# Local attention and a feed-forward block on one core: split values, means and maxima go through a buffer in HBM, and four more chunks use seven block products

## The chip, the cores and the metric

The kernel runs on one core of a Trainium2 chip. The metric is the device time of one execution in microseconds (us): the median of 3 runs is 672.36 us (671.85 to 673.94). Beside them stands one execution under the profiler. The five engines are called as in the profile: PE multiplies matrices (PEld is its weight load), DVE, ACT and POOL work on vectors, and SP issues the DMA transfers of this kernel, one after the other.

## The reference

The inputs are q, k, v with 4 batches, 8 heads, 768 positions and 64 columns a head, and two weights. Per head, each query attends to the keys closer than 16 positions and, without a mask, to one maximum of the keys and one mean of the values for every block of 32. The heads side by side are then the 512 columns of 3072 tokens of a feed-forward block.

```
k_sum = k.reshape(B, H, nb, 32, D).max(axis=3)
v_sum = v.reshape(B, H, nb, 32, D).mean(axis=3)
scores = concat([where(|i - j| < 16, scale*q@k.T, -1e9), scale*q@k_sum.T + log(32)])
a = softmax(scores)                      # over keys and block maxima together
x = a @ concat([v, v_sum])               # (B, H, S, D) -> (3072, 512)
h = x @ w_in                             # 512 -> 2048
out = (h * sigmoid(h)) @ w_out           # 2048 -> 512
```

## The kernel before

**Number format.** Chunk 0 of the tokens multiplies in float32. Everything later is scaled by a power of two and split into two float16 parts, high and low, and each product is three float16 matmuls (high by high, high by low, low by high). The scale comes from a maximum over all 128 partitions: `all_max`, a reduction on POOL over the partitions. It is used once for the weights (`w_scale`), once per batch for the values (`v_scale`) and once each for batches 1 to 3 for queries and keys (`job_scale`).

**Attention.** The 3072 tokens are 24 tiles `s` of 128 queries, 6 to a batch. A tile goes through `job_qk` (load and split q and k), `job_scores` (PE, line 605), `job_a` (softmax on DVE and ACT, then four DMA transposes, line 691, that turn the probabilities), `job_c` (PE, line 724, the product with the values) and `job_x` (split x). For `job_c` each half tile `z` of 64 queries needs one tile `vv` in SBUF with 96 rows of local values and 24 rows of block means, each row 512 columns high and 512 low in float16, 2 KB. In batches 1 to 3, which are 18 tiles, `job_vn` loads 256 rows of v, splits them on ACT or DVE (lines 545 to 547) into one of two slots `vn`, and `job_vs` then copies rows from the slots and from `vmp` (the means) to `vv` by eight DMAs from SBUF to SBUF, all issued at line 574: of 15, 81, 79 and 17 rows, and four of 24 rows. A slot can be written again when the copies that read it have landed.

**Feed-forward.** Twelve chunks of 256 tokens. A chunk takes the 2048 hidden columns in eight pairs of 128. In chunks 1 to 9 a pair (`job_f`) is 24 matmuls of 256 columns (line 838), a chain of ACT and DVE (lines 863 to 867) and 12 matmuls of 512 columns (line 851). In chunks 10 and 11 (`FAST = 10`) the second product of a pair (`job_fast`) is made of seven block products with 21 matmuls of 256 columns (line 968). For it, DVE or POOL form four sums of 128 columns (line 953), and two more splits follow (lines 949, 950, 955, 956).

**Order.** A planner (`Plan`) receives every operation with its engine, cost, buffers and priority, sweeps through them with modelled latencies and writes one fixed order per engine. Each engine works through its list in that order, so an instruction that waits holds back all that stand behind it on its engine. Attention for chunk `c + 2` is placed among the products of chunk `c`. The table `TUNE` shifts the priorities. Where the planner sees PE idle early or ahead of a first product it puts in matmuls on an identity (line 337).

Of the kernel before, what the change touches and what calls it, by code (L numbers as in the profile page):

```python
# [10 lines left out]
F32 = mybir.dt.float32  # L11
# [45 lines left out]
NSUP = 2  # L57
FAST = 10
EARLY = 40
ALLMAX = 1100  # L60
PACE = 4
# [6 lines left out]
class Plan:  # L68
# [58 lines left out]
    def sweep(self, prio, on, back):  # L127
# [18 lines left out]
        while ready:  # L146
# [13 lines left out]
            if e == "pe" and not back:  # L160
                early = early and cols < self.BUSY
# [12 lines left out]
            else:  # L174
                stop = t + cost * (1.0 if e in ("pe", "dma") else self.MARGIN)
# [58 lines left out]
def local_attn_ffn(ctx: ExitStack, tc: tile.TileContext, qkT, qP, qF, kF, v, vR, vP, w, out):  # L234
# [17 lines left out]
    const = ctx.enter_context(tc.tile_pool(name="const", bufs=1))  # L252
    psum = ctx.enter_context(tc.tile_pool(name="psum", bufs=1, space=bass.MemoryType.PSUM))

# [50 lines left out]
    v0_t = ring(2, [P, 2 * DM], F32, "v0")  # L305
    vn_t = [t.bitcast(F16).rearrange("p (a i c) -> p a i c", a=2, i=2) for t in v0_t]
    vmf_t = const.tile([P, 4, P], F16, name="vmf")
    nc.gpsimd.memset(vmf_t, 0.0)
# [28 lines left out]
    plan = Plan(tc, lambda: nc.tensor.matmul(out=bank[0][:, :2 * P], lhsT=unit[:, :P], rhs=unit, start=True, stop=True))  # L337
    count = {}

    def nxt(tag, n):  # L340
# [16 lines left out]
    def bk(k):  # L357
        return [("bank", k, half) for half in range(2)]
# [33 lines left out]
    def job_scale(b, prio):  # L392
# [8 lines left out]
        qs = qsc_t[b % 2]  # L401
        plan.op({"pool": ALLMAX}, lambda e: all_max(qc[:, 0:2], qm_t[:, 7:9]), r=["qm_q", "qm_k"], w=["qc"], prio=prio)
        steps = (
# [9 lines left out]
    def job_km(b, prio):  # L413
# [30 lines left out]
    def job_v(b, prio):  # L444
# [14 lines left out]
        plan.op({"dve": 180}, lambda e: nc.vector.scalar_tensor_tensor(out=lo, in0=vm_t, scalar=by, in1=hi, op0=ALU.mult, op1=ALU.subtract), r=need, w=["vmf"], prio=prio)  # L459
        plan.op({"dma": 1250}, lambda e: nc.sync.dma_start_transpose(out=vmp_t, in_=vmf_t.rearrange("p a b -> p (a b)")), r=["vmf"], w=["vmp"], prio=prio)  # L460

# [77 lines left out]
    def job_vn(b, n, prio):  # L539
# [6 lines left out]
                nc.vector.tensor_scalar(out=vn[:, :, 0], in0=flat, scalar1=vsc[:, 0:1], scalar2=None, op0=ALU.mult), r=key + [("vsc", b % 2)], w=vn_key(g % 2), prio=prio)  # L546
        plan.op({"dve": 1196}, lambda e: nc.vector.scalar_tensor_tensor(out=vn[:, :, 1], in0=flat, scalar=vsc[:, 0:1], in1=vn[:, :, 0], op0=ALU.mult, op1=ALU.subtract), r=key + [("vsc", b % 2)], w=vn_key(g % 2), prio=prio)

    def job_vs(s, prio):
        prio += nudge("vs", s)  # L550
        b, t = divmod(s, NTILE)
        if b == 0:
            return
        if t == 0:
            job_vn(b, 0, prio)
            job_vn(b, 1, prio)
        if t == 3:
            job_vn(b, 2, prio)
        vv = vv_t[s % 2]
        key = ("vv", s % 2)  # L560

        def rows(z, at, tile, first, n):
            if not 0 <= tile < NTILE:
                return vv[at:at + n, z].rearrange("p i c -> p (i c)").bitcast(F32), v[0, t if z == 0 else NTILE - 1, at:at + n, z, :]
            g = (b - 1) * (NTILE // 2) + tile // 2
            return vv[at:at + n, z], vn_t[g % 2][first:first + n, tile % 2]
# [9 lines left out]
        slots = {((b - 1) * (NTILE // 2) + x // 2) % 2 for x in (t - 1, t, t + 1) if 0 <= x < NTILE}  # L576
        plan.op({"dma": 2100}, load, r=["vmp", "first"] + [k for x in slots for k in vn_key(x)], w=[key], prio=prio)

# [44 lines left out]
    def job_a(m, prio):  # L623
# [55 lines left out]
        for j, n in enumerate(ns):  # L679
# [10 lines left out]
            plan.op({"dve": 510}, low, r=[sum_key(j, i) for i in range(2)] + [("e", n, i) for i in range(2)], w=pkeys, prio=prio)  # L690
            plan.op({"dma": 1250}, lambda e, tt=tt, pt=pt: nc.sync.dma_start_transpose(out=tt, in_=pt.rearrange("p a b -> p (a b)")), r=pkeys + ["third"], w=[ttk], prio=prio)

# [98 lines left out]
    def w_scale(prio):  # L791
        plan.op({"dve": 80}, lambda e: nc.vector.tensor_reduce(out=wx_t, in_=wm_t, axis=AX.X, op=ALU.max), r=[("wm", f, kind) for f in range(NFT) for kind in range(2)], w=["wx"], prio=prio)
        plan.op({"pool": ALLMAX}, lambda e: all_max(wc[:, 0:2], wx_t), r=["wx"], w=["wc"], prio=prio)
        steps = (
# [18 lines left out]
    def job_f(n, c, fs):  # L813
# [11 lines left out]

        def fill():
            nc.tensor.matmul(out=h[:, :CH], lhsT=unit[:, :P], rhs=unit, start=True, stop=True)

        def ffn1(at, f, cs):
# [25 lines left out]
        for at, f in enumerate(fs):  # L855
            need = [("wf", f, 0)] if c == 0 else [("wh", f, 0), ("wl", f, 0)]
            if n < HALVES:
                for half in range(2):
                    cs = slice(half * P, half * P + P)
                    plan.op({"pe": 900}, ffn1(at, f, cs), r=[("xh", z, half), ("xl", z, half)] + need, w=[("bank", k, half)], prio=i, cols=2048, fill=fill)  # L860
            else:
                plan.op({"pe": 1800 if c == 0 else 1312}, ffn1(at, f, slice(0, CH)), r=xs + need + turn, w=bk(k) if at == 0 else [("bank", k, 1)], prio=i + at, cols=4096 if c == 0 else 3072, fill=fill)
        plan.op({"act": 51 + 213 * m if c == 0 else 147 + 213 * m}, lambda e: nc.scalar.activation(out=t, in_=h, func=AF.Tanh, scale=0.5 if c == 0 else th[:, 0:1]), r=bk(k) + ([("th", b % 2)] if c else []) + free, w=tk, prio=post)  # L863
# [65 lines left out]
    def job_fast(n, c, fs):  # L929
# [6 lines left out]

        def fill():
            nc.tensor.matmul(out=h[:, :CH], lhsT=unit[:, :P], rhs=unit, start=True, stop=True)

        for at, y in enumerate(fs):  # L940
            plan.op({"pe": 1312}, ffn1_pairs(h, at, y, z), r=[(x, z, half) for x in ("xh", "xl") for half in range(2)] + [("wh", y, 0), ("wl", y, 0), ("turn", n - 3)], w=bk(k) if at == 0 else [("bank", k, 1)], prio=i + at, cols=3072, fill=fill)
        t = area(4 * j + 3, 0, F32)
# [70 lines left out]
    def job_tail(n, c, fs):  # L1013
# [8 lines left out]

        def fill():
            nc.tensor.matmul(out=h[:, :CH], lhsT=unit[:, :P], rhs=unit, start=True, stop=True)

        for at, f in enumerate(fs):
            plan.op({"pe": 1312}, ffn1_pairs(h, at, f, z), r=[(x, z, half) for x in ("xh", "xl") for half in range(2)] + [("wh", f, 0), ("wl", f, 0), ("turn", n - 3)], w=bk(k) if at == 0 else [("bank", k, 1)], prio=i + at, cols=3072, fill=fill)
        for at in range(2):
# [130 lines left out]

TUNE = dict(quad=308.75, vd=-86.5, ws=818.0, s0=-738.75, wp=1594.25, wm=33.0, km=-55.75, w_dma=-1.5, w_dec=878.75, a0=-71.0, a1=-119.25, d1=-66.5, span=51.75, post=1866.5, ffn2=5.0, jc0=92.5, jc1=-1748.25, jx0=2.25, jx1=143.0, vs=617.5, qk=305.75, k=-1369.75, v=-54.75, v0=83.75, out=-4.5, first=1452.5)  # L1160

# [60 lines left out]
```

## Time and profile before

| | before |
|---|---|
| median of 3 runs | 672.36 us |
| profiled execution, device time | 674.95 us |
| its span, first to last instruction | 673.2 us |
| PE busy | 598.7 us, 89% |
| DVE busy | 458.7 us, 68% |
| ACT busy | 342.6 us, 51% |
| POOL busy | 92.9 us, 14% |
| mean granted PE clock | 0.953 of full speed |

The span is what the rows below divide; the device time of the same execution is 1.75 us longer. A busy PE need not work at its peak, since the granted clock may be at its lower level. The three stages used later are the start with chunks 0 and 1 (0 to 126 us), chunks 2 to 9 with most of the attention (126 to 584 us), and chunks 10 and 11 (584 us to the end).

### The profile page before, as it was taken

To read this page: it belongs to the slowest core of one execution; us is meant where nothing else is said; L and a number is where in the kernel's file an instruction comes from. 1 tells how busy PE (TensorE), PEld (TensorE's weight loads), DVE (VectorE), ACT (ScalarE), POOL (GpSimd) and SP (SyncE) were. 2 spreads that over 40 slices of the span, in tenths; PEclk is the share of its full clock that TensorE was granted. 3 is DMA by queue.
4 is the path that set the end of the run, shared out by engine and by line. 5 is a ranking of instruction groups with operands and counts; after the bars stand their busy time and mean duration, and the time that the engine had idled before them with its cause. 6 is when DMAs were issued, how large, how long until landed. Compare 5 with 4: busy or idle time off the path is not lost.

```text
span 673.2 us, 15159 instructions
## 1 busy us (share of the span) xinstructions
PE 598.7 (89%) x5944; PEld 413.3 (61%) x5944; DVE 458.7 (68%) x1243; ACT 342.6 (51%) x837; POOL 92.9 (14%) x183
## 2 busy tenths in 40 slices
PE   8899999799749858996998876999996798999997
PEld 5667666466526525663665543666663566688886
DVE  6799897898074636982773643879857696255655
ACT  4899885565054541651554532545643554234342
POOL 4112002201000000000000000005222420031130
PEclk9999999799969969998999797999997899999999
DMA  8997612237544539636433536474473379000000
GB/s 342 417 418 284 201 56 87 77 101 92 117 129 124 118 123 140 157 81 83 127 98 101 144 72 97 109 183 44 141 78 103 46 88 80 1 32 1 33 1 31
DMA packets 64938, 80.07 MB, mean 119 GB/s; under 512 B 44068, under 2 KB 46052, under 8 KB 63076
## 3 DMA queue, kind: packets, MB, share of 16 engines
q1 hardware_dynamic: 64868, 79.12, 48.0%
q8 instruction: 46, 0.75, 0.5%
q14 instruction: 24, 0.20, 0.1%
HBM read 54.33 MB, written 6.29 MB: 90 GB/s over the span
## 4 chain that ended last, share of the span: by engine, by line
PE 46%; DMA 21%; DVE 15%; ACT 9%; SPq 4%; issue 4%; POOL 0%; DVEq 0%; ACTq 0%
PE bank L851 16%; PE bank L838 15%; DMA first<-v 9%; PE bank L926 6%; DMA raw<-in_qF_dram 6%; PE bank L968 5%; SPq L574 3%; DMA third<-first 2%; DVE wr L789 2%; ACT e L644 2%; DVE wr L773 2%; PE bank L724 1%; PE bank L605 1%; ACT wr L866 1%; DVE first L688 1%
## 5 line engine op out<-in xcount | busy, mean ns | idle before, releaser
L851 PE MATMUL bank<-wr 128*128 128x512 f16 x768 | 193.1, 400 | 52.6 <-ACT wr L866 45.2
L838 PE MATMUL bank<-x,wr 128*128 128x256 f16 x1728 | 205.2, 275 | 1.3 <-DVE work L864 1.3
L838 PEld LDWEIGHTS <-wr 128*128 128x128 f16 x1728 | 169.3, 99 | 38.8 <-issue 3.7
L851 PEld LDWEIGHTS <-wr 128*128 128x128 f16 x768 | 75.0, 101 | 140.3 <-ACT wr L866 47.2
L864 DVE SCALAR_TENSOR_TENSOR wr<-wr,bank 128x512 f32<-128x512 f32 x64 | 43.7, 683 | 67.0 <-ACT wr L863 66.7
L644 ACT ACTIVATE e<-e,mx 128x120 f32<-128x120 f32 x192 | 73.2, 384 | 17.4 <-DVE mx L641 17.3
L863 ACT ACTIVATE wr<-bank,th 128x512 f32<-128x512 f32 x64 | 43.5, 679 | 69.2 <-PE bank L838 69.2
L866 ACT ACTIVATE wr<-wr 128x512 f16<-128x512 f32 x64 | 40.1, 627 | 49.4 <-DVE wr L864 49.3
L867 DVE SCALAR_TENSOR_TENSOR wr<-wr 128x512 f16<-128x512 f32 x64 | 45.9, 717 | 16.1 <-ACT wr L866 15.7
L688 DVE SCALAR_TENSOR_TENSOR first<-e,sum,first 128x120 f16<-128x120 f32 x144 | 44.9, 363 | 4.3 <-POOL first L657 4.1
L657 POOL TENSOR_SCALAR first<-e,sum 128x120 f16<-128x120 f32 x33 | 14.9, 455 | 238.2 <-DVE sum L650 56.4
L926 PE MATMUL bank<-x,wr 128*128 128x256 f16 x384 | 45.8, 273 | 0.1
L641 DVE CUSTOM_DVE_ANT_0 e<-bank,masks,qsc 128x120 f32<-128x120 f32 x144 | 40.2, 338 | 4.5 <-PE bank L605 4.5
L926 PEld LDWEIGHTS <-wr 128*128 128x128 f16 x384 | 37.5, 98 | 5.5 <-issue 0.3
L968 PE MATMUL bank<-wr 128*128 128x256 f16 x315 | 37.7, 273 | 0.0
L644 ACT ACTIVATION_READ_ACCUMULATOR e<-e,mx 128x1 f32 x192 | 36.5, 190 | 0.0
L968 PEld LDWEIGHTS <-wr 128*128 128x128 f16 x315 | 30.7, 98 | 3.6
L848 PE MATMUL bank<-wr,work 128*128 128x512 f32 x64 | 29.2, 594 | 1.6 <-DVE work L864 1.6
L835 PE MATMUL bank<-x,wr 128*128 128x256 f32 (+1 forms) x144 | 29.8, 359 | 0.4 <-issue 0.4
L953 POOL TENSOR_TENSOR wr<-wr 128x128 f32<-128x128 f32 x33 | 18.8, 573 | 76.0 <-DVE wr L953 71.0
L250 POOL TENSOR_TENSOR wr<-wr 128x256 f32<-128x256 f32 x32 | 25.8, 823 | 20.4 <-DVE wr L911 11.6
L851 PE MATMUL bank<-wr,work 128*128 128x512 f16 x96 | 24.2, 395 | 4.7 <-ACT work L866 2.7
(153 smaller groups left out, 760.8 us busy)
## 6 DMA issues: line engine op xcount, KB each, us to landing
wr<-in_w_dram SPq DMA_DIRECT2D x14, 1024.0 KB
raw<-in_qkT_dram SPq DMA_DIRECT2D x18, 576.0 KB
out_dram<-raw SPq DMA_DIRECT2D x23, 256.0 KB
raw<-in_kF_dram SPq DMA_DIRECT2D x12, 384.0 KB
raw<-in_qF_dram SPq DMA_DIRECT2D x9, 512.0 KB
raw<-in_vR_dram SPq DMA_DIRECT2D x12, 384.0 KB
raw<-in_vP_dram SPq DMA_DIRECT2D x9, 512.0 KB
first<-v SPq DMA_DIRECT2D x18, 162.0 KB
```

The lines of the kernel that those rows point to most:

```text
L641: plan.op({"dve": 262 if b else 206}, lambda e, i=i, j=j, et=et, mx=mx: nc.vector.tensor_tensor_reduce(out=et[:, i, :], in0=sc[j][:, i, :N ...
L644: plan.op({"act": 385}, lambda e, i=i, j=j, et=et, mx=mx: nc.scalar.activation(out=et[:, i, :], in_=et[:, i, :], func=AF.Exp, scale=-1.0, ...
L688: nc.vector.scalar_tensor_tensor(out=pt[:, i, P:P + NKEY], in0=et[:, i, :], scalar=su4[:, 2 * j + i:2 * j + i + 1], in1=pt[:, i, :NKEY], o ...
L835: nc.tensor.matmul(out=o, lhsT=wi[:, ct * P:(ct + 1) * P], rhs=x0[:, ct, cs], start=(ct == 0), stop=(ct == NCT - 1))
L838: nc.tensor.matmul(out=o, lhsT=wip[:, part, ct * P:(ct + 1) * P], rhs=x[:, ct, :], start=(ct == 0 and q == 0), stop=(ct == NCT - 1 and q = ...
L851: nc.tensor.matmul(out=bank[ob[u]][:, cs], lhsT=g[:, rows], rhs=wop[:, part, cs], start=(begins and q == 0), stop=(stops and q == 2))
L863: plan.op({"act": 51 + 213 * m if c == 0 else 147 + 213 * m}, lambda e: nc.scalar.activation(out=t, in_=h, func=AF.Tanh, scale=0.5 if c == ...
L864: plan.op({"dve": 70 + 267 * m}, lambda e: nc.vector.scalar_tensor_tensor(out=t, in0=t, scalar=1.0, in1=h, op0=ALU.add, op1=ALU.mult), r=b ...
L866: plan.op({"act": 98 + 213 * m}, lambda e: nc.scalar.activation(out=gh, in_=t, func=AF.Copy, scale=SHRINK), r=tk + free, w=ghk, prio=post)
L867: plan.op({"dve": 76 + 267 * m}, lambda e: nc.vector.scalar_tensor_tensor(out=gl, in0=t, scalar=SHRINK, in1=gh, op0=ALU.mult, op1=ALU.subt ...
L926: nc.tensor.matmul(out=h[:, at * CH:at * CH + CH], lhsT=wip[:, p, ct * P:(ct + 1) * P], rhs=x[:, ct, :], start=(ct == 0 and q == 0), stop= ...
L968: nc.tensor.matmul(out=acc_of(c, m)[0], lhsT=x[:, left[m]], rhs=right[m](p), start=(opens and q == 0 and m in (1, 4, 2, 7)), stop=(closes ...
```

## The change

- **Values.** After the split, `job_vn` stores 256 rows from its slot to `vd` in HBM (line 564). `job_vs` then reads the local rows of each half tile from there with one DMA of up to 96 rows (line 592), so two per tile in place of four. The means are stored once per batch to `md` in HBM by `keep` (two DMAs, line 474) and read into each of the two `vv` buffers once per batch (line 581).
- **Maxima.** `all_max` no longer runs on POOL. It stores the 128 partitions' values to `sd` in HBM (line 430), reads them back into every partition (line 431) and reduces on DVE (line 432). This is done eight times.
- **Chunks.** `FAST = 6`: chunks 6 to 9 also take their second product by seven block products.
- **Order.** Some costs given to the planner change, its rule for early identity matmuls changes, and `TUNE` has other numbers, so the order of all engines is another one.

```
-FAST = 10
+FAST = 6
...
-    def all_max(out, in_):
-        nc.gpsimd.partition_all_reduce(out, in_, P, bass_isa.ReduceOp.max)
...
+    def all_max(out, in_, r, w, prio):
+        i, n = nxt("sd", 2 * B), in_.shape[1]
+        flat, row = sd_t[i].rearrange("p n -> (p n)")[:n * P], vms_t[:, :n * P]
+        plan.op({"dma": 600}, lambda e: nc.sync.dma_start(out=flat.rearrange("(p n) -> p n", n=n), in_=in_), r=r, w=[("sd", i)], prio=prio)
+        plan.op({"dma": 450}, lambda e: nc.sync.dma_start(out=row, in_=flat.unsqueeze(0).to_broadcast([P, n * P])), r=[("sd", i)], w=[("vms", 0)], prio=prio)
+        plan.op({"dve": 65 + 133 * n}, lambda e: nc.vector.tensor_reduce(out=out, in_=row.rearrange("q (p n) -> q n p", n=n), axis=AX.X, op=ALU.max), r=[("vms", 0)], w=w, prio=prio, port=())
...
+        def keep(e):
+            for i in range(2):
+                nc.sync.dma_start(out=md_t[b - 1][:, i], in_=vmp_t[i * BLK:i * BLK + NB].rearrange("p a b -> p (a b)"))
...
+        plan.op({"dma": 1300}, lambda e: nc.sync.dma_start(out=vd_t[b - 1][n * 2 * P:(n + 1) * 2 * P].rearrange("(a p) i c -> p a i c", a=2), in_=vn), r=vn_key(g % 2), w=[("vd", b, n)], prio=prio)
...
-        part = P - HALF + HALO
-        moves = [rows(0, NB, t - 1, P - HALO, HALO), rows(0, NB + HALO, t, 0, part + 2), rows(1, 0, t, HALF - HALO, part), rows(1, part, t + 1, 0, HALO + 2)]
-        moves += [(vv[rowsm[z], z, i], vmp_t[i * BLK:i * BLK + NB].rearrange("p a b -> p (a b)")) for z in range(2) for i in range(2)]
...
-            for o, i in moves:
-                nc.sync.dma_start(out=o, in_=i)
...
-        plan.op({"dma": 2100}, load, r=["vmp", "first"] + [k for x in slots for k in vn_key(x)], w=[key], prio=prio)
...
+            a = t * P + z * HALF - HALO
+            lo, hi = max(a, 0), min(a + NKEY - NB, S)
+            spans.append((local[z].start + lo - a, lo, hi))
...
+            for z, (at, lo, hi) in enumerate(spans):
+                nc.sync.dma_start(out=vv[at:at + hi - lo, z], in_=vd_t[b - 1][lo:hi])
...
+        plan.op({"dma": 1050}, load, r=[("vd", b, n) for n in units] + ["first"], w=[key], prio=prio)
```

On SP, this is what one tile's copies look like before, about a third of the way through (`v_125` and `v_126` are the two slots, `first` holds `vv`, and the last number of rows times 1024 columns is the size):

```order
L691 DMA_TRANSPOSE third<-first 128x4x128 x4
L574 DMA first<-v_126 15x1024
L574 DMA first<-v_126 81x1024
L574 DMA first<-v_126 79x1024
L574 DMA first<-v_125 17x1024
L574 DMA first<-vmp 24x512 x4
L377 DMA raw_117<-in_kF_dram 128x768
L397 DMA raw_116<-in_qF_dram 128x1024
```

And here is SP after, at the end of the first of the three batches, where the maxima for the next batch pass through HBM (`sd`) and the last tile of the batch reads its rows from `vd`:

```order
L430 DMA sd_139<-qm 128x2
L431 DMA vms<-sd_139 128x256
L592 DMA first<-vd_129 96x1024
L592 DMA first<-vd_129 79x1024
L459 DMA raw_120<-in_vR_dram 128x768
L709 DMA_TRANSPOSE third<-first 128x4x128
L459 DMA raw_120<-in_vR_dram 128x768
L709 DMA_TRANSPOSE third<-first 128x4x128 x3
```

Eight issues for a tile have become two. Over the program SP issues 30 loads of 96 rows, 3 of 81 and 3 of 79; one of 79 is the last tile of each batch, whose halo ends at the last position.

The other place is DVE at the scale of the weights. Before, `wc` comes straight behind `wx`, from POOL:

```order
L864 SCALAR_TENSOR_TENSOR work<-work,bank_170 128x512
L792 TENSOR_REDUCE wx<-wm 128x2
L795 TENSOR_SCALAR wc<-wc 128x2
L796 TENSOR_SCALAR wc<-wc 128x2
L797 TENSOR_SCALAR ws<-wc 128x2
L798 RECIPROCAL ws<-ws 128x2
```

After, five instructions of other work stand between `wx` and the reduction that reads the values back:

```order
L810 TENSOR_REDUCE wx<-wm 128x2
L381 TENSOR_REDUCE km_151<-raw_119 128x24
L760 SCALAR_TENSOR_TENSOR x_182<-bank_192,vsc_157,x_182 128x4x128
L381 TENSOR_REDUCE km_151<-raw_120 128x24
L879 SCALAR_TENSOR_TENSOR work<-work,bank_185 128x512
L381 TENSOR_REDUCE km_151<-raw_119 128x24
L432 TENSOR_REDUCE wc<-vms 128x2
L813 TENSOR_SCALAR wc<-wc 128x2
```

The reductions of the keys' blocks, which stood ahead of `wx` before, have moved behind it.

Counted over the whole program, DVE has 1246 instructions after and 1245 before; scalings of probabilities on DVE (line 659) fall from 71 to 27, with more of them on ACT and POOL, and the four sums of a pair stand 160 times on POOL after and 33 times before.

## Rows read from the trace of the kernel before

**Rows 1.** Stages by windows: us, busy time (count) per engine, granted clock, DMA share, GB/s.
```profile
0.00:126.00 126.00, 114.13 (x1034) 78.09 (x1035) 110.50 (x262) 97.81 (x216) 24.79 (x67) 0.99 0.64 241
126.00:584.00 458.00, 399.35 (x4128) 262.50 (x4127) 299.22 (x890) 212.39 (x568) 49.30 (x83) 0.94 0.53 105
584.00:673.20 89.20, 85.25 (x787) 72.69 (x784) 48.93 (x91) 32.44 (x55) 18.77 (x33) 0.99 0.05 19
```

**Rows 2.** Pieces of the chain that ended last: durations of PE groups at full clock.
```profile
536.21 2.59 PE bank L851 x12
...
544.86 2.62 PE bank L838 x24
...
617.70 2.29 PE bank L968 x21
```

**Rows 3.** The stretch of 126 to 584 us by line 838 alone: PE and PEld busy (count).
```profile
126.00:584.00 458.00, 188.31 (x1584) 155.25 (x1584) 0.94 0.53 105
```

**Rows 4.** The same by line 851 alone.
```profile
126.00:584.00 458.00, 198.59 (x790) 76.76 (x788) 0.94 0.53 105
```

**Rows 5.** Timeline, PE only: the product with the values and the scores of a tile.
```profile
165.82 0.95 PE L724 MATMUL bank<-third,first 120*64 120x64 f16 x48
...
171.37 0.82 PE L605 MATMUL bank<-second 64*64 64x120 f16 x48
```

**Rows 6.** Waits of PE in 126 to 584 us: total us, times, longest.
```profile
PE bank L851 <- ACT wr L866: 45.2, 8, 13.1
...
PE bank L851 <- DVE wr L867: 7.3, 5, 4.4
PE bank L724 <- DMA third<-first: 5.9, 4, 3.6
```

**Rows 7.** Pieces of the same chain that are transfers: start, us, what.
```profile
106.65 3.56 DMA raw<-in_qF_dram
...
166.33 10.44 DMA first<-v
...
233.62 9.43 DMA raw<-in_qF_dram
...
258.20 3.38 DMA raw<-in_vR_dram
...
362.74 7.69 DMA raw<-in_kF_dram
...
384.58 12.02 DMA first<-v
398.40 2.19 DMA first<-vmp
```

**Rows 8.** Timeline around the longest idle time of PE: SP issues, DVE and PE.
```profile
182.78 3.22 SPq L574 DMA_DIRECT2D first<-v  x4
...
186.05 3.42 SPq L574 DMA_DIRECT2D first<-vmp  x4
...
188.53 0.76 DVE L546 TENSOR_SCALAR v<-raw,vsc 128x1024 f16<-128x1024 f32 x1 [16.20 <-DMA first<-v]
```

**Rows 9.** A window in which ACT waits for the load of 233.62 us.
```profile
239.60:243.00 3.40, 0.00 (x1) 0.00 (x0) 0.00 (x0) 0.00 (x0) 0.00 (x0) 0.84 0.07 26
```

**Rows 10.** The maximum for the weights on POOL and its reader on DVE, timeline.
```profile
77.33 0.38 POOL L247 PARTITION_ALL_REDUCE wc<-wx  x1 [12.16 <-DVE wx L792]
...
77.74 0.17 DVE L795 TENSOR_SCALAR wc<-wc 128x2 f32<-128x2 f32 x1 [0.62 <-POOL wc L247]
```

**Rows 11.** Groups by line: vector work of a pair, the plain way and by seven products.
```profile
L867 DVE SCALAR_TENSOR_TENSOR wr<-wr 128x512 f16<-128x512 f32 x64 | 45.9, 717 | 16.1 <-ACT wr L866 15.7
...
L953 POOL TENSOR_TENSOR wr<-wr 128x128 f32<-128x128 f32 x33 | 18.8, 573 | 76.0 <-DVE wr L953 71.0 <-DVE wr L945 3.9
...
L950 DVE SCALAR_TENSOR_TENSOR wr<-wr 128x384 f16<-128x384 f32 x15 | 10.9, 728 | 0.7
...
L956 DVE SCALAR_TENSOR_TENSOR wr<-wr 128x512 f16<-128x512 f32 x15 | 10.4, 691 | 12.5 <-ACT wr L955 12.4
```

More of the change, by code (lines that the diff above doesn't have):

```diff
@@ L6 @@
 import concourse.tile as tile
-from concourse import bass_isa, mybir
+from concourse import mybir
 from concourse.masks import make_identity
@@ L160, in sweep @@
             if e == "pe" and not back:
-                early = early and cols < self.BUSY
+                early = early and not self.ops[i][6]
                 if early or self.ops[i][6]:
@@ L252, in local_attn_ffn @@
     const = ctx.enter_context(tc.tile_pool(name="const", bufs=1))
+    far = ctx.enter_context(tc.tile_pool(name="far", bufs=1, space=bass.MemoryType.DRAM))
     psum = ctx.enter_context(tc.tile_pool(name="psum", bufs=1, space=bass.MemoryType.PSUM))
@@ L306, in local_attn_ffn @@
     vn_t = [t.bitcast(F16).rearrange("p (a i c) -> p a i c", a=2, i=2) for t in v0_t]
+    vd_t = [far.tile([S, 2, DM], F16, name=f"vd{i}") for i in range(B - 1)]
+    md_t = [far.tile([NB, 2, DM], F16, name=f"md{i}") for i in range(B - 1)]
+    sd_t = [far.tile([P, 2], F32, name=f"sd{i}") for i in range(2 * B)]
     vmf_t = const.tile([P, 4, P], F16, name="vmf")
@@ L338, in local_attn_ffn, with idle @@
     count = {}
+    def idle(o):
+        return lambda: nc.tensor.matmul(out=o, lhsT=unit[:, :P], rhs=unit[:, :o.shape[1]], start=True, stop=True)
     def nxt(tag, n):
@@ L935, in job_fast @@
         h = bank[k]
-        def fill():
-            nc.tensor.matmul(out=h[:, :CH], lhsT=unit[:, :P], rhs=unit, start=True, stop=True)
         for at, y in enumerate(fs):
-            plan.op({"pe": 1312}, ffn1_pairs(h, at, y, z), r=[(x, z, half) for x in ("xh", "xl") for half in range(2)] + [("wh", y, 0), ("wl", y, 0), ("turn", n - 3)], w=bk(k) if at == 0 else [("bank", k, 1)], prio=i + at, cols=3072, fill=fill)
+            plan.op({"pe": 1312}, ffn1_pairs(h, at, y, z), r=[(x, z, half) for x in ("xh", "xl") for half in range(2)] + [("wh", y, 0), ("wl", y, 0), ("turn", n - 3)], w=bk(k) if at == 0 else [("bank", k, 1)], prio=i + at, cols=3072, fill=idle(h[:, at * CH:at * CH + CH]))
         t = area(4 * j + 3, 0, F32)
@@ L1021, in job_tail @@
         release("tail", tk + ghk + glk, post)
-        def fill():
-            nc.tensor.matmul(out=h[:, :CH], lhsT=unit[:, :P], rhs=unit, start=True, stop=True)
         for at, f in enumerate(fs):
-            plan.op({"pe": 1312}, ffn1_pairs(h, at, f, z), r=[(x, z, half) for x in ("xh", "xl") for half in range(2)] + [("wh", f, 0), ("wl", f, 0), ("turn", n - 3)], w=bk(k) if at == 0 else [("bank", k, 1)], prio=i + at, cols=3072, fill=fill)
+            plan.op({"pe": 1312}, ffn1_pairs(h, at, f, z), r=[(x, z, half) for x in ("xh", "xl") for half in range(2)] + [("wh", f, 0), ("wl", f, 0), ("turn", n - 3)], w=bk(k) if at == 0 else [("bank", k, 1)], prio=i + at, cols=3072, fill=idle(h[:, at * CH:at * CH + CH]))
         for at in range(2):
@@ L1157, in local_attn_ffn @@
     plan.issue()
-TUNE = dict(quad=308.75, vd=-86.5, ws=818.0, s0=-738.75, wp=1594.25, wm=33.0, km=-55.75, w_dma=-1.5, w_dec=878.75, a0=-71.0, a1=-119.25, d1=-66.5, span=51.75, post=1866.5, ffn2=5.0, jc0=92.5, jc1=-1748.25, jx0=2.25, jx1=143.0, vs=617.5, qk=305.75, k=-1369.75, v=-54.75, v0=83.75, out=-4.5, first=1452.5)
+TUNE = dict(quad=-30.75, vd=-11.0, ws=-845.5, s0=3027.0, wp=623.75, wm=55.75, km=703.75, w_dma=27.5, w_dec=-2.75, a0=490.0, a1=-2168.0, d1=201.25, span=75.25, post=3599.25, ffn2=753.0, jc0=-1061.5, jc1=716.0, jx0=-191.25, jx1=1364.5, vs=765.0, qk=-243.25, k=-423.0, v=1879.25, v0=-41.25, out=1280.75, first=65.75)
 NUDGE = {}
```

45 lines of the change are left out of this document (22 added, 23 removed).

## The prediction

> **What bounds the kernel now.** I read the stages first [rows 1]. Each row gives the length of a stage, then busy time per engine, PE's granted clock and the share of the DMA engines. From 584 us on, PE is busy 85.25 of 89.2 us at a clock of 0.99: there PE's columns set the time. In the first 126 us DVE is busy 110.5 us, and PE 114.13. [...]
>
> [...] A group of 24 first-product matmuls takes 2.62 us when nothing disturbs it, one of 12 second-product matmuls 2.59 us [rows 2]. The stretch holds 1584 of the first and 790 of the second [rows 3, 4], so 1584 / 24 x 2.62 = 172.9 us and 790 / 12 x 2.59 = 170.5 us. To this come attention's products, 0.95 and 0.82 us a tile [rows 5], for about 17 and 18 tiles: 30.9 us. Together 374.3 us, and 458 - 374.3 = 83.7 us are lost: the 58.65 idle ones and 25 at the lower clock after them.
>
> Whom does PE wait for? The waits of PE [rows 6] are to be read with the chain, because the engine they name is only the last link: line 851 waits 45.2 us for ACT and 7.3 us for DVE, and line 724 waits 5.9 us for the transposes. The chain [rows 7] shows what stood behind it. A 512 KB load of q lands in 3.56 us and a load of v in 3.38 us where no copies to `vv` are under way. Where copies stand ahead of them, a load of q takes 9.43 us and one of k 7.69, and the copies themselves 10.44 and 12.02 us. The longest idle time of PE shows how that gets to PE [rows 8]: SP issues eight copies of line 574, 3.22 + 3.42 us for the issuing alone, DVE waits 16.20 us at line 546 to overwrite a slot that copies still read, the splits of the feed-forward block stand behind that instruction on DVE, and PE gets its next second product 13 us late. I went through PE's gaps one by one. Six of the eight that end with ACT (42 us), the one of 4.4 us that ends with DVE and the 5.9 us at line 724 lie behind such a late transfer: 52.3 of 58.65 us, or 89%.
>
> Why are the copies slow? While ACT waits for the q load of 233.62 us, PE, DVE, ACT and POOL stand still, and the DMA engines are at a share of 0.07, moving 26 GB/s [rows 9]. A share of 0.07 is 1.1 engines of 16. So part of what is queued runs on one engine, and a load that is spread over all has to wait for its share on that one. The copies of 79 and 17 rows are 158 + 34 = 192 KB; at 26 GB/s they are 7.4 us, about what the late loads are late by (9.43 - 3.56 = 5.9).
>
> [...]
>
> **The change, part by part.**
>
> *Seven products in chunks 6 to 9.* 32 pairs replace 2.59 us by 21 matmuls in 2.29 us [rows 2]: 32 x 0.30 = **-9.6 us** of PE. On DVE a pair gains a split of 384 columns (0.728 us) and has one of 0.691 in place of 0.717 [rows 11], together 22.5 us more; 44 scalings of probabilities leave DVE in the new order. POOL takes most of the four sums, 4 x 0.573 = 2.3 us a pair. The cover is DVE's and POOL's idle time in the stretch, 159 and 409 us [rows 1]. I take 0. If the cover is gone, each us that a pair waits is 32 us; that is a rival below.
>
> *Values through HBM.* Each of 18 tiles loses eight issues of about 0.8 us on SP [rows 8] and gets two (four for the first two tiles of a batch); per batch come three stores of 512 KB and two of means. With 36 loads, 12 of means, 9 and 6 stores in place of 144 copies, SP issues 81 fewer, 65 us of its time. The new path has one hop more, store and then load. Bounds for a hop: 2.19 us, a copy of 24 KB [rows 7], and 3.56 us, a 512 KB load. Two hops are 4.4 to 7.1 us against 10.4 to 12 us now. What the loads do to others is the main term. If they spread over all engines, the 89% of the loss go: 0.89 x 83.7 = **-74.5 us**. If they don't, nothing goes. I take the spread, since 512 KB in 3.56 us is 147 GB/s, over five times what one engine moves [rows 9]. Three loads of 79 rows are left, and I let them stay as slow as the copies were: 3 x 74.5 / 18 x 158 / 192 = **+10 us** (from 0, if other work hides them, to 3 x 6.2 = 18 us, their whole time on one engine).
>
> *Order.* The stores wait on SP for DVE's split, and behind them stand transposes. That can cost what the copies cost; it is in the third case below.
>
> *Maxima through HBM.* The reduction on POOL and the wait for it are 0.62 us before the reader on DVE starts [rows 10]. A store and a load back are 2 x 2.19 = 4.4 us, so 3.8 us more, eight times. For the weights this lies on the path to chunk 1, whose splits all wait for that scale; five other instructions on DVE fill the gap, which were due anyway, but ACT's splits start later. Bounds 0 to 3.8; I take **+2 us**. The other seven are ahead of their readers by other work in the order; uncovered they are up to 7 x 3.8 = 27 us. I take 0.
>
> *The sum.* The profiled span is 673.2 us: 673.2 - 9.6 - 74.5 + 10 + 2 = 601.1. That execution's device time is 1.75 us over its span and 2.6 us over the median of the runs, so the median comes to 601.1 + 1.75 - 2.6 = 600.3. **I predict 600 us.** About 9 us of the old loss stay in it.
>
> **The rivals.**
>
> *All of the loss goes.* The loads of 79 rows are hidden, and the rest of the waits goes as well, because it was only pushed along by the late transfers: 673.2 - 9.6 - 83.7 - 0.85 = 579 us. For it: behind 584 us, where nothing is copied, PE is 96% busy. Against it: waits that have nothing to do with copies, as the 2 us ones among the eight in [rows 6], come up as soon as larger ones are gone.
>
> *A new wait takes half of it back.* Chunks 6 to 9 now have a longer chain on ACT, DVE and POOL beside attention, or SP's stores hold back transposes. One us per pair in four chunks is 32 us, half of the 74.5 is 37: some 632 to 637 us. For it: with seven products PE needs the sums and a second pair of splits before its last products, and the 33 sums on POOL already waited 71 us for DVE [rows 11]. Against it: chunks 10 and 11 have that chain and lose 4 us in 16 pairs [rows 1], though without attention.
>
> *The new loads run on one engine too.* Then the bytes decide: a tile's two loads are 2 x 192 = 384 KB, 14.8 us on one engine at 26 GB/s in place of 7.4, and the loss about doubles: 672 - 9.6 + 2 + 74.5 = 739 us. It is slower than before from a time on one engine of about 8.2 us a tile on (1.1 times 7.4, where the 7.6 us gained elsewhere are used up). Against it speaks the rate of the q load, for it that no trace here has a transfer of 96 rows.
>
> *The order makes the gain void.* The whole order is a new one, and attention could be late for each chunk as it is now, whatever the transfers do: 672 - 9.6 + 2, about 665 us. Nothing in the trace speaks for it beyond that waits were there before.
>
> **How the numbers follow.** The sum above, 588 to 616 us around the bounds of its small terms: 0.47. All goes, below 588: 0.24. Half comes back, 616 to 645: 0.21. Void, 645 to 670: 0.03. One engine or another loss: 0.05. From 577 to 640 us about 2 in 10 are left out: the upper end of the third case, the last two, and what would be below 577. Runs of this kernel spread by 0.3%, about what a measurement can tell from no change. The first four cases are faster by more than that: 0.94, with 0.01 of the void case taken as the same; slower 0.05.
>
> **What would show it.** In the changed kernel's chain, pieces of line 592 of 2 to 4 us in place of 10 to 12, and loads of q and k at 3.5 us; the stretch of chunks 2 to 9 with under 20 us of idle PE; DVE no longer waiting at the split of v; a window with a DMA share near 0.07 only behind the three loads of 79 rows; 21 matmuls in 2.29 us in chunks 6 to 9. The prediction is wrong if transfers are quick and PE still waits, above all for the sums of line 965 or for an instruction of DVE that waits for line 431, or if a share of 0.07 is seen behind 96 rows.

## The result, and the profile of the changed kernel

The changed kernel takes 618.07 us (median of 4 runs, 616.9 to 619.31) and the kernel before 672.48 us on the same chip. The ratio is 0.9188, with a 95% interval of 0.9161 to 0.9215. The forecast was 600 us with a range of 577 to 640: the time lies inside, 18 us above the likeliest value. In two of the experiments one execution stands apart, 642.56 us of `max_on_pool` at a clock of 0.923 and 1534.13 us of `before_spread`, both without a known cause: the ratios leave them out, the medians count them.

The stages, the same view as [rows 1], with one more row for the tiles' stretch up to 527 us, where chunk 10 begins now. The profiled span is 617.2 us.

```profile
0.00:126.00 126.00, 113.06 (x1039) 77.03 (x1039) 100.73 (x258) 95.78 (x220) 26.96 (x64) 0.99 0.71 247
126.00:584.00 458.00, 437.64 (x4938) 338.51 (x4939) 352.17 (x955) 263.88 (x669) 138.37 (x245) 0.97 0.47 115
...
126.00:527.00 401.00, 380.64 (x4298) 287.87 (x4299) 315.55 (x869) 238.09 (x612) 120.69 (x212) 0.97 0.52 126
```

In the 458 us of chunks 2 to 9 PE is now idle for 458 - 437.64 = 20.4 us in place of 458 - 399.35 = 58.65, and the granted clock rose from 0.94 to 0.97. Before, no engine was full there, with PE busy for 399 us of the 458, DVE for 299 and ACT for 212 [rows 1], so the stretch was bound by waits; and the clock stood at 0.50 from 184 to 197 us, in the longest idle time of PE and for 3 us behind it. Much of the lost time came back, but behind 126 us PE still stops in three places for 4 to 7 us and in a fourth for 2. The waits of PE and of DVE, total us, times, longest:

```profile
PE bank L623 <- DVE mx L659: 6.9, 2, 6.7
PE bank L866 <- DVE sc L441: 4.9, 1, 4.9
PE bank L866 <- ACT wr L881: 4.4, 1, 4.4
...
PE bank L980 <- DVE sc L442: 2.0, 1, 2.0
```

```profile
DVE sc L432 <- DMA vms<-sd: 26.4, 4, 8.4
...
DVE am L462 <- DMA raw<-in_vR_dram: 10.1, 3, 6.6
...
DVE qc L432 <- DMA vms<-sd: 4.8, 3, 2.9
```

Line 432 is the reduction that reads a maximum back from HBM. DVE stands still ahead of it eight times out of eight, 32.1 us in all, as the summary of the line's waits says (us, times):

```profile
  DMA vms<-sd: 32.1, 8
```

The timeline of the largest case (start, us, engine, line; in brackets the idle time and who ended it) shows how that reaches PE:

```profile
139.85 0.14 DVE L435 TENSOR_REDUCE am<-am 128x1 f32<-128x4 f32 x1
...
140.02 0.33 SPq L430 DMA_DIRECT2D sd<-am  x1
...
147.71 0.33 SPq L431 DMA_DIRECT2D vms<-sd  x1
...
153.48 0.29 DVE L432 TENSOR_REDUCE sc<-vms 128x1 f32<-128x128 f32 x1 [7.04 <-DMA vms<-sd]
...
155.79 0.30 PE L623 MATMUL bank<-second 64*64 64x120 f16 x1 [6.66 <-DVE mx L659]
```

From `am` to the reader 13.6 us pass. DVE had other work for 6.4 us of them, then it waits for 7.04, and the masked scores (line 659) and the chain of the feed-forward block stand behind line 432 on DVE, so PE stops for 6.66 us. Two more of PE's waits, for `sc` at lines 441 and 442, have the same source. The 4.4 us at line 866 are another matter and come up in the second experiment. The transfers of the chain that ended last, answering to [rows 7]:

```profile
81.89 4.52 DMA sd<-wx
86.43 4.18 DMA vms<-sd
...
140.02 7.67 DMA sd<-am
147.71 5.75 DMA vms<-sd
...
211.80 3.32 DMA raw<-in_kF_dram
...
232.89 10.86 DMA raw<-in_vR_dram
...
269.17 8.45 DMA sd<-am
277.64 5.71 DMA vms<-sd
...
369.48 6.43 DMA raw<-in_qF_dram
...
378.48 4.06 DMA sd<-qm
382.55 4.31 DMA vms<-sd
...
413.46 3.49 DMA raw<-in_vR_dram
...
419.34 8.87 DMA sd<-am
428.23 5.24 DMA vms<-sd
```

No load of line 592 is left in that chain, and none of PE, DVE or ACT waits for one. One hop of a maximum takes 4.1 to 8.9 us in these rows. The very first store, among the loads of the start, where the DMA engines are at a share of 0.89 (30 to 47 us), took longer still:

```profile
30.09 16.67 DMA sd<-am
```

DVE is not the only engine that stands still. The load back waits on SP until the store has landed, so SP issues nothing from 140.35 to 147.71 us, and whatever stands behind it in SP's list is late as well. This is SP's own row for the four maxima of the values (total us, times, longest):

```profile
SPq L431 <- DMA sd<-am: 35.3, 4, 13.6
```

### The profile page after: what moved, and what is told of

It is laid out like the page before. It is cut to its first block, busy times and chain, and to the rows that moved or that the text cites. A ratio compares the mean times of both kernels' runs of the same rounds, so it can differ in the third digit from the quotient of the medians.

```text
span 617.2 us, 15861 instructions
## 1 busy us (share of the span) xinstructions
PE 580.0 (94%) x6235; PEld 440.7 (71%) x6235; DVE 470.3 (76%) x1244; ACT 369.8 (60%) x906; POOL 170.4 (28%) x318
## 4 chain that ended last, share of the span: by engine, by line
PE 50%; DMA 27%; DVE 15%; ACT 5%; issue 2%; POOL 0%; SPq 0%; DVEq 0%; ACTq 0%
PE bank L941 15%; PE bank L980 13%; PE bank L866 9%; PE bank L853 8%; DMA sd<-am 7%; DMA vms<-sd 5%; DMA wr<-in_w_dram 3%; DMA raw<-in_vR_dram 2%; DMA wr<-in_v_dram 2%; PE bank L742 2%; DMA out_dram<-raw 2%; DVE e L659 1%; PE bank L623 1%; DMA sd<-qm 1%; DVE wr L807 1%
## 5 line engine op out<-in xcount | busy, mean ns | idle before, releaser
L965 POOL TENSOR_TENSOR wr<-wr 128x128 f32<-128x128 f32 x160 | 88.2, 568 | 146.8 <-DVE wr L957 67.1
L941 PEld LDWEIGHTS <-wr 128*128 128x128 f16 x1152 | 112.5, 98 | 14.4
L980 PE MATMUL bank<-wr 128*128 128x256 f16 x987 | 119.3, 276 | 3.6 <-DVE sc L442 2.0
L980 PEld LDWEIGHTS <-wr 128*128 128x128 f16 x987 | 96.5, 99 | 17.2 <-DVE sc L442 2.3
L853 PEld LDWEIGHTS <-wr 128*128 128x128 f16 x960 | 93.7, 98 | 19.8 <-issue 0.9
L866 PE MATMUL bank<-wr 128*128 128x512 f16 x384 | 93.3, 390 | 9.3 <-DVE sc L441 4.9
L866 PEld LDWEIGHTS <-wr 128*128 128x128 f16 x384 | 36.9, 100 | 49.7 <-DVE sc L441 5.4
L956 ACT ACTIVATE wr<-bank,th 128x512 f32<-128x512 f32 x47 | 32.0, 682 | 36.6 <-PE bank L941 36.4
L957 DVE SCALAR_TENSOR_TENSOR wr<-wr,bank 128x512 f32<-128x512 f32 x47 | 32.0, 682 | 27.3 <-ACT wr L956 27.3
L968 DVE SCALAR_TENSOR_TENSOR wr<-wr 128x512 f16<-128x512 f32 x47 | 33.7, 716 | 16.6 <-ACT wr L967 16.5
L967 ACT ACTIVATE wr<-wr 128x512 f16<-128x512 f32 x47 | 29.3, 623 | 26.4 <-POOL wr L965 26.3
L878 ACT ACTIVATE wr<-bank,th 128x512 f32<-128x512 f32 x32 | 21.8, 681 | 34.5 <-PE bank L853 34.3
L961 ACT ACTIVATE wr<-wr 128x384 f16<-128x384 f32 x47 | 24.4, 520 | 28.7 <-DVE wr L957 28.5
L962 DVE SCALAR_TENSOR_TENSOR wr<-wr 128x384 f16<-128x384 f32 x47 | 31.1, 662 | 4.7 <-ACT wr L961 3.8
```

The costliest lines, as they stand in the source:

```text
L853: nc.tensor.matmul(out=o, lhsT=wip[:, part, ct * P:(ct + 1) * P], rhs=x[:, ct, :], start=(ct == 0 and q == 0), stop=(ct == NCT - 1 and q = ...
L866: nc.tensor.matmul(out=bank[ob[u]][:, cs], lhsT=g[:, rows], rhs=wop[:, part, cs], start=(begins and q == 0), stop=(stops and q == 2))
L941: nc.tensor.matmul(out=h[:, at * CH:at * CH + CH], lhsT=wip[:, p, ct * P:(ct + 1) * P], rhs=x[:, ct, :], start=(ct == 0 and q == 0), stop= ...
L956: plan.op({"act": 573}, lambda e: nc.scalar.activation(out=t, in_=h, func=AF.Tanh, scale=th[:, 0:1]), r=bk(k) + [("th", b % 2), "areas"], ...
L957: plan.op({"dve": 604}, lambda e: nc.vector.scalar_tensor_tensor(out=t, in0=t, scalar=1.0, in1=h, op0=ALU.add, op1=ALU.mult), r=bk(k), w=t ...
L962: plan.op({"dve": 470}, lambda e: nc.vector.scalar_tensor_tensor(out=ld, in0=src, scalar=SHRINK, in1=hd, op0=ALU.mult, op1=ALU.subtract), ...
```

## The experiments

All but two (`fast_10` and `max_on_dve_planned`) keep the planned order of the kernel that they start from, so that only the edited piece differs. The kernel before runs at 671.46 to 671.81 us beside them.

### The maxima on POOL again

`max_on_pool` gives `all_max` its old reduction back. The two transfers stand in the plan as before and issue nothing.

```
-plan.op({"dma": 600}, lambda e: nc.sync.dma_start(out=flat..., in_=in_), ...)
-plan.op({"dma": 450}, lambda e: nc.sync.dma_start(out=row, in_=flat...), ...)
+plan.op({"dma": 600}, lambda e: None, ...)
+plan.op({"dma": 450}, lambda e: None, ...)
-plan.op({"dve": ...}, lambda e: nc.vector.tensor_reduce(out=out, in_=row..., op=ALU.max), ...)
+plan.op({"dve": ...}, lambda e: nc.gpsimd.partition_all_reduce(out, in_, P, bass_isa.ReduceOp.max), ...)
```

> The changed kernel with its planned order kept on every engine, but the eight maxima over partitions are again formed on POOL in place of the store to HBM, the load back and the reduction on DVE. Theory 1 (DVE standing at line 432 for the load back, 32.1 us in all, is the largest loss left): the PE gaps behind it, 2.2 + 6.7 + 0.3 + 4.9 + 2.0 + 0.5 = 16.6 us, and some low clock after them go: 596 to 602 us, with no DVE wait over 4 us at the reader. Theory 2 (those waits only take up slack, and PE then waits for the next late thing): 612 us or more.

Measured: 633.85 us, ratio 0.9421 [0.9368, 0.9475]. It is slower than the changed kernel, as the second theory has it, so the 0.62 us that the prediction put on the reduction on POOL were wrong as well. The timeline of one reduction:

```profile
281.25 0.38 POOL L430 PARTITION_ALL_REDUCE sc<-am  x1 [5.83 <-issue]
281.66 0.15 DVE L439 TENSOR_SCALAR sc<-sc 128x1 f32<-128x1 f32 x1 [5.69 <-POOL sc L430]
...
288.67 1.51 POOL L246 TENSOR_TENSOR wr<-wr 128x256 f32<-128x256 f32 x2 [7.04 <-issue]
...
290.22 1.15 ACT L922 ACTIVATE wr<-wr,ws 128x1024 f16<-128x1024 f32 x1 [12.28 <-POOL wr L246]
```

The reduction itself is 0.38 us. POOL waits for nothing that the profile shows for 5.83 us before it and for 7.04 us before its next instruction. The operations of line 430 name what stands there, and those of line 246 show the same behind a reduction, ahead of the ordinary work that follows:

```profile
L430 POOLq MODIFY_POOL_CONFIG  x16: 4/6/13, 47.1 to 435.3; - x16
```

```profile
L246 POOLq MODIFY_POOL_CONFIG  x4: 83/83/83, 237.7 to 281.6; - x4
```

Sixteen of the first for eight reductions, two ahead of each. In the trace of the kernel before, with sixteen at line 247, sixteen more stand behind its eight reductions, at the lines of POOL's next work: 14 at line 657 and two at line 250. So POOL's configuration is changed there and back (the expectations call it POOL's code). No instruction of the traces shows the 5.83 and the 7.04 us as work of POOL, and neither was in the forecast in any form. Both stood in the trace of the kernel before too, as in these two rows of POOL:

```profile
116.06 0.37 POOL L247 PARTITION_ALL_REDUCE qc<-qm  x1 [5.90 <-issue]
...
254.74 0.35 POOL L657 TENSOR_SCALAR first<-e,sum 128x120 f16<-128x120 f32 x1 [7.46 <-issue]
```

But POOL was idle in most of the stretch [rows 1], so DVE waited for the reductions 7.4 us in all, 0.62 of them at the one in [rows 10]. With four sums of each pair on POOL, 13 us of POOL at a time are no longer free.

### The loads of 79 rows

`split_79` issues each of the three loads of 79 rows as 64 and 15.

```
+                cut = lo + 64 if hi - lo == 79 else hi
-                nc.sync.dma_start(out=vv[at:at + hi - lo, z], in_=vd_t[b - 1][lo:hi])
+                nc.sync.dma_start(out=vv[at:at + cut - lo, z], in_=vd_t[b - 1][lo:cut])
+                if cut < hi:
+                    nc.sync.dma_start(out=vv[at + cut - lo:at + hi - lo, z], in_=vd_t[b - 1][cut:hi])
```

> The changed kernel with its order, but each of the three loads of 79 rows is issued as one of 64 and one of 15 rows. Theory 1 (79 rows run on one DMA engine and hold up the load of v issued behind them, 10.86 us at 232.89 us, and with it PE for 4.36 us): that load lands in 3 to 5 us, no window behind it shows a DMA share of 0.13 at 25 GB/s, and the time falls by 3 to 8 us, to 610 to 615. Theory 2 (other work hides these loads): 616 to 619 us, unchanged.

Measured: 608.56 us, ratio 0.9069 [0.9009, 0.9128], 9.5 us less, a little more than expected; its four executions lie from 605.62 to 611.89 us. In the changed kernel the load `raw<-in_vR_dram` of 232.89 us stood right behind a load of 79 rows and took 10.86 us. DVE waited for it for 6.65 us and PE for 4.36 us. Where ACT and DVE stand nearly still there, the DMA engines move 25 GB/s, the rate of [rows 9] (us, busy time of the engines, clock, share, GB/s):

```profile
238.00:243.50 5.50, 5.50 (x41) 3.79 (x39) 0.00 (x0) 0.69 (x1) 0.52 (x1) 1.00 0.13 25
```

With 64 and 15 rows that load takes 5.77 us, near the expected 3 to 5, and PE's gap is 0.35 us. From 126 to 584 us PE is idle for 12.9 us in place of 20.4, at a clock of 0.99 in place of 0.97. The two mends at once, `pool_and_split`:

> Both at once: maxima on POOL and the loads of 79 rows split, in the changed kernel's order. If the two losses are apart, the gains add: 590 to 598 us. If one hides the other, no less than the better of the two alone.

Measured: 632.17 us, ratio 0.9404 [0.9361, 0.9448], not to be told from `max_on_pool` alone. Where POOL's changes of configuration set the time, the split gives nothing that can be told from noise.

### The maxima with two columns

Batches' values store one column, 4 bytes a partition; queries, keys and weights store two. In the chain above the first kind takes 7.67 to 8.87 us, the second 4.06 and 4.52. `max_two_columns` stores two columns for the values as well.

```
-        all_max(sc2[:, 0:1], am_t[:, 7:8], ["am4"], ["sc2"], prio)
+        all_max(sc2, am_t[:, 6:8], ["am4"], ["sc2"], prio, 65 + 133)
```

> The changed kernel with its order, but the four maxima for the values are stored to HBM as two columns (8 bytes a partition, one of them unused) and not one (4 bytes a partition). The maxima for queries and keys, already two columns, took 4.1 to 4.7 us for the store, those of one column 7.7 to 8.9 us at a DMA share of 0.04 to 0.07. Theory 1 (one column runs on one DMA engine in very small pieces): the stores fall to 4 to 5 us, DVE waits some 4 x 3.5 = 14 us less at line 432, and the time falls by 7 to 13 us, to 605 to 611. Theory 2 (the stores are slow because of loads ahead of them): stores and time as they were, 616 to 619 us.

Measured: 597.14 us, ratio 0.889 [0.8845, 0.8935], 21 us less than the changed kernel, by doubling the bytes of four small stores. It is more than either theory expected: not only DVE's wait goes down, but SP's wait ahead of line 431 too, and the runs don't tell the two apart. The same places in its chain:

```profile
136.80 2.96 DMA sd<-am
139.78 4.71 DMA vms<-sd
...
261.41 4.34 DMA sd<-am
265.76 5.67 DMA vms<-sd
```

The idle time of DVE at the line falls from 32.1 us to 13.9. `columns_and_split` adds the split loads:

> The changed kernel with both mends that helped alone: maxima of the values stored as two columns, and the loads of 79 rows issued as 64 + 15. If the two are independent: 618 - 21 - 9.5 = 587.5 us, 583 to 592. If the same waits carried both, the larger alone: about 596 us.

Measured: 593.9 us, ratio 0.8841 [0.8821, 0.886]. The interval overlaps that of two columns alone, so the 3 us that the split still gives there are not settled by the times, which are nearer to the forecast of "the larger alone". In the traces the split still does its part: the gap of PE at the second product that ends with ACT is 4.6 us with two columns alone and 0.7 us with both.

### No maxima over the partitions

`max_left_out` puts a copy on POOL in the place of the reduction of `max_on_pool`, so each partition keeps its own maximum and the maximum over partitions is left out.

```
+plan.op({"dve": ...}, lambda e: copy("pool", out, in_), ...)
```

> As max_on_pool, but the reduction over the partitions is left out: a copy on POOL takes its place, so each partition keeps its own maximum (this part of the computation is left out). The order stays. Theory 1 (max_on_pool lost its time in changing POOL's code around each reduction, 5.8 us before and 7.0 after): without the change of code the time falls far below that of the changed kernel, 580 to 592 us. Theory 2 (max_on_pool lost it because POOL's place in the order is too late for the readers): 615 to 634 us as there. The difference of the changed kernel to this run is what all its maxima cost.

Measured: 582.57 us, ratio 0.8679 [0.8663, 0.8695]. The readers and their place in the order are those of `max_on_pool`; its kernel has no reduction on POOL (the trace of the changed kernel, which has none either, shows no MODIFY_POOL_CONFIG after the first us), and 51 us are gone, of which the reductions' own time is 8 x 0.38 = 3 us. So what stands around them was the cost there, and the maxima through HBM cost the changed kernel 618.07 - 582.57 = 35.5 us, DVE's waits and SP's together. Its stretches:

```profile
126.00:527.00 401.00, 400.52 (x4681) 312.74 (x4680) 330.29 (x909) 251.95 (x650) 136.57 (x241) 1.00 0.49 128
...
126.00:584.00 458.00, 449.38 (x5118) 355.42 (x5116) 360.25 (x964) 269.42 (x680) 146.69 (x259) 1.00 0.44 115
```

The span ends at 579.8 us, inside the second window. Up to 527 us PE is idle for 0.5 us, and the clock stands at 1.00: in this run PE hardly waits and doesn't lose its clock either. No gap of PE over 0.35 us is left behind 126 us, though the loads of 79 rows are as in the changed kernel.

### Row counts, from both sides

`before_spread` is the kernel before, with each of its copies of 79 rows issued as 64 and 15, and each of 17 as 16 and 1.

```
+                cut = {79: 64, 17: 16}.get(n, n)
-                nc.sync.dma_start(out=o, in_=i)
+                nc.sync.dma_start(out=o[:cut], in_=i[:cut])
+                if cut < n:
+                    nc.sync.dma_start(out=o[cut:], in_=i[cut:])
```

> [...] Theory 1, the prediction's (the loss in chunks 2 to 9 comes from rows that are queued on one DMA engine): a large part of the 74.5 us goes, 600 to 635 us. Theory 2 (what counts is that a copy goes from SBUF to SBUF, or the time that eight issues take on SP): two more issues of 0.8 us a tile, 672 to 690 us.

Measured: 638.22 us, ratio 0.9502 [0.9484, 0.9519], 33 us less than the kernel before and 3 us above the range of the first theory. `after_one_engine` goes the other way: every load of values in the changed kernel is issued as 79 rows and the rest.

```
+                cut = min(lo + 79, hi)
```

> The changed kernel, but each load of 96 and 81 rows of values issued as 79 rows and the rest, so that 158 to 192 KB of each half tile go over one engine if the row count decides. Theory 1: a tile has some 384 KB on one engine, 14.8 us at 26 GB/s, twice what it had before: the loss of chunks 2 to 9 comes back and grows, 680 to 760 us. Theory 2 (the path through HBM is the gain, whatever the rows): one more issue on SP a load, 618 to 630 us.

Measured: 777.62 us, ratio 1.1566 [1.1533, 1.1599], more than the 739 us of the prediction's rival and above both ranges. A window in one of these loads, and what SP's issues of the rows behind the 79 take (min, median, max in ns):

```profile
176.00:178.00 2.00, 2.00 (x17) 1.47 (x16) 1.83 (x6) 0.63 (x1) 0.00 (x0) 1.00 0.07 26
```

```profile
L595 SPq DMA_DIRECT2D first<-vd x33: 498/5445/7510, 173.3 to 687.0; - x33
```

A share of 0.07 and 26 GB/s, as in [rows 9], now through HBM and with the same bytes that go without harm as 96 rows. The second row is what the forecast lacked. The issue of the few rows behind 79 keeps SP for 5.4 us in the median, and all of the other transfers stand behind it on SP. So the 160 us hold both the slow loads and SP's time, and the run doesn't separate them.

What was left in `before_spread` was tried next: `before_spread_means_once` issues the four copies of means for the first two tiles of a batch only.

```
+        if t < 2:
             moves += [(vv[rowsm[z], z, i], vmp_t[i * BLK:i * BLK + NB]...) for z in range(2) for i in range(2)]
```

> As before_spread, and the four copies of means (24 rows each) are issued for the first two tiles of a batch only, since their rows stay in the two buffers: 12 tiles lose four issues of 0.72 us on SP, 35 us of SP's time in all. Theory 1 (what before_spread left of the loss is SP's issuing, late for the tiles): from 638 to 615 to 630 us. Theory 2 (it is the copies' time, or waits of the order): 634 to 640 us.

Measured: 617.39 us, ratio 0.9181 [0.9157, 0.9205]. The kernel before, with its own path from SBUF to SBUF, its maxima on POOL and `FAST = 10`, reaches the time of the changed kernel by another choice of rows and fewer copies. Whether the 21 us of this step are SP's time for issuing or the time of the copies themselves isn't told apart, since both go together.

### The seven products, and a maximum without transfers

`fast_10` is the changed kernel with one number put back.

```
-FAST = 6
+FAST = 10
```

> The changed kernel with chunks 6 to 9 multiplied the plain way again (FAST = 10), the rest of the change kept; the order is planned anew. Theory 1 (the seven products give 32 pairs x 0.30 us and their extra work on DVE and POOL lies beside PE): 618 + 9.6 = 628 us, and some us either way from the new order. Theory 2 (the extra sums and splits make new waits that cost as much): 610 to 619 us.

Measured: 630.11 us, ratio 0.9363 [0.9314, 0.9412]: 12.0 us more than the changed kernel. `max_on_dve` forms the maxima on DVE alone, with split loads of 79 rows:

```
+            nc.vector.transpose(out=s, in_=in_.unsqueeze(2).to_broadcast([P, n, BLK]))
+            nc.vector.tensor_reduce(out=m, in_=s..., op=ALU.max)
+            for step in (HALF, BLK):
+                for at in range(0, P, step):
+                    nc.vector.tensor_copy(out=o[at:at + step], in_=m[at ^ step:(at ^ step) + step])
+                nc.vector.tensor_tensor(out=m if step == HALF else out, in0=m, in1=o, op=ALU.max)
```

> The changed kernel's order, the loads of 79 rows issued as 64 + 15, and the maxima over the partitions formed on DVE alone: a transpose of 32 x 32 blocks, a reduction, two rounds of moves between the four groups of 32 partitions, ten small instructions with no transfer and no change of POOL's code. If the waits for the maxima are what columns_and_split still has over a kernel without maxima: max_left_out's 582.6, less up to 9.5 us of the split loads, plus 8 x 1 us of DVE: 575 to 586 us. If the ten instructions on DVE hold back what stands behind them: 590 us and more.

Measured: 588.86 us, ratio 0.8756 [0.8733, 0.8778], the fastest kernel here that keeps the whole computation, 29 us below the changed one. One maximum:

```profile
47.86 0.20 DVE L432 STREAM_TRANSPOSE wide<-am 128x32 f32<-128x32 f32 x1
48.09 0.18 DVE L433 TENSOR_REDUCE wide<-wide 128x1 f32<-128x32 f32 x1
48.31 0.31 DVE L436 COPY wide<-wide 64x1 f32<-64x1 f32 x2
48.66 0.16 DVE L437 TENSOR_TENSOR wide<-wide 128x1 f32<-128x1 f32 x1
48.85 0.62 DVE L436 COPY wide<-wide 32x1 f32<-32x1 f32 x4
49.51 0.16 DVE L437 TENSOR_TENSOR sc<-wide 128x1 f32<-128x1 f32 x1
```

1.8 us from the first to the last, against 13.6 us for the two transfers above. It misses the expected 575 to 586 by 3 us, for which no cause was tested. The planner was then told of it:

> As max_on_dve, but the planner is told that a maximum takes 1.9 us of DVE and no transfers, so the whole order is planned anew for it. If the old order, which leaves time for two transfers that are gone, still costs something: 575 to 587 us. If a new order only moves the small waits about: 587 to 600 us; the distance from 588.9 is then also how much an order planned anew is worth by chance, which bears on fast_10.

Measured: 589.0 us, ratio 0.8779 [0.8754, 0.8804], no difference. The old order was no handicap, and in this one case an order planned anew was worth 0.1 us; what it was worth in `fast_10` is not known.

## Why the prediction was right, and where it was not

| term, us | predicted | measured | from |
|---|---|---|---|
| seven products | -9.6 | -12.0 | `fast_10` |
| transfers of values, with the loads of 79 rows | -64.5 | -76.9 | `max_left_out` |
| maxima | +2 | +35.5 | `max_left_out` |
| sum on 672 | 600 | 618 | |

The second measured term is 582.57 - 671.46 + 12.0, what is left when the others are taken off, so the column adds up by its making. It holds the new order, which no run takes by itself, and can hold a few us of the old maxima, for which DVE waited 7.4 us in all before. That 618 lies inside the range is in part luck: 33.5 us too little for the maxima stand against 14.8 too little gain from the other two terms. The order of `fast_10` was planned anew, and DVE waits 36.7 us for maxima there in place of 32.1, so some 5 of the 12 us may be these.

**The step that failed** is that of the maxima: a hop of 2.19 us from a row of 24 KB, and "the other seven are ahead of their readers by other work in the order", taken as 0 with 27 us if uncovered. A hop took 4.1 to 8.9 us in the rows of the chain above, and a maximum 8.4 to 14.2 in place of 4.4, without the first, whose store took 16.67. The order did put other work ahead of the readers, 6.4 us of it in the timeline above, which is more than 4.4 and far less than 13.6. None of the eight was covered in full. The weights, the one that I charged, made DVE wait for 0.9 us of the 32.1. Even the bound of 27 was too low. The prediction's last paragraph named an instruction that waits for line 431 as what would make it wrong; it is just that.

**The price of what was removed** was also misread. POOL's 0.62 us [rows 10] was what DVE noticed, not what POOL spent. Putting the reduction back showed 5.8 and 7.0 us around 0.38. So the removal was worth it, as 633.85 against 618.07 us show: in the changed kernel, with four sums a pair on POOL, the old way is worse still.

**The main term held in size, and its mechanism is shown for a part.** The cause that it named is one engine's worth of bandwidth behind 79 and 17 rows. Taking the rows apart in the kernel before gave 33 us, and issuing the means less often another 21; putting 79 rows into the changed kernel cost 160, SP's held issues among them. Of the 76.9 us some 23 are left that no run takes apart: the path through HBM, the rest of the issues and the new order are in them. That the 0.07 of [rows 9] belongs to 79 and 17 rows, and that 79 rows would go on so in the new loads (the +10 us), was the prediction's estimate from bytes and a rate; no run had shown it, nor how 96 rows go. The trace of the changed kernel shows 96 and 79 rows. Two loads of 96 rows, issued at 501.72 us when the DMA engines stood still (a share of 0.00 from 499 to 501 us), bring them to a share of 0.92 at 315 GB/s from 503 to 504 us, and from 505 to 507 us it is 0.00 again. Behind the last pair, of 96 and 79 rows, issued at 527.87 us, it is 0.07 at 19 GB/s from 530 to 532 us, and 0.07 at 29 from 534 to 536. No run shows 17 rows by themselves. Two corrections. First, the row count is shown to be worth 33 us, with two more issues a tile; fewer copies of the means, and with them fewer of the issues that I counted as 65 us of SP's time but did not price, are the next 21. Second, more was gained than 89% of the loss: with the maxima gone nearly all of it goes, as the rival of 579 us said.

**The loads of 79 rows** were put at +10 us; taking them apart gave 9.5. That is near by its size, which is luck: the prediction took three equal shares, and only one of the three was seen to stop PE. With the values' maxima mended the split gave 3 us, within the intervals, and without maxima no gap stands behind these loads.

**What would show it.** 21 matmuls of line 980 take 2.29 us, no piece of line 592 is in the chain, and DVE no longer waits at the split of v: as said. PE is idle for 20.4 us from 126 to 527 us where "under 20" stood: just missed. Loads of q and k at 3.5 us: some, but the one of 369.48 us took 6.43. A DMA share near 0.07 only behind 79 rows: no, it also stands behind a store of one column (last section).

Of the rivals, the "new wait that takes half of it back" was nearest in size (632 to 637 us), but not in place: it named SP's stores and the sums of seven products. `fast_10` shows no such loss.

## What to carry to other kernels

When a wait of 0.6 us is read from a trace, look also at what the engine did before and after it: work that is hidden by an idle engine comes up as soon as the engine gets other work, as 5.8 and 7.0 us did here on POOL. Stores of 512 bytes took 7.7 us and more here and a copy of 24 KB 2.19, so the bytes don't give the price of a small transfer: take it from one of the same direction and layout, twice if it goes there and back, and check the cover of every instance in the order, not of one. And look at the row count and the number of DMAs before their path: these two were worth 54 us in the kernel before, whose copies stayed in SBUF.

## What the runs showed of the hardware that was not expected

In the chain of the changed kernel, stores of one column, 4 bytes a partition, took 7.67, 8.45 and 8.87 us behind the start, those of two columns 4.06 to 4.68. The one of 7.67 us ran with the DMA engines at a share of 0.06 and 4 GB/s:

```profile
141.00:147.00 6.00, 6.00 (x85) 4.05 (x84) 5.39 (x9) 2.32 (x5) 0.64 (x2) 1.00 0.06 4
```

That is about one engine of 16 in use. In the same places stores of two columns took 2.96 and 4.34 us in `max_two_columns`, and the share was 0.08 at 3 GB/s from 137 to 139.7 us, so about one engine as well: the share doesn't tell the two apart. Why one column takes longer is not settled: no run varied the layout of the small buffer in HBM.

An SP issue can be held: in `after_one_engine` it took 0.36 us in the median for 79 rows, and 5.4 us for the rows issued right behind them. What it waits for is not shown. It is not so wherever 17 rows follow 79: in the kernel before, no copy from the slots took more than 1.44 us to issue at line 574.
